# Natural order of the model dimension, and half of the input tiles transposed by DMA, in a fused spectral and GEGLU backward pass

## The chip, the cores and the metric

The kernel runs on one core of one Trainium2 chip. The metric is the device time of one execution in microseconds (us). The core has TensorE (PE in the profile, with its weight loads as PEld), VectorE (DVE), ScalarE (ACT), GpSimd (POOL) and SyncE (SP). SP computes nothing: it issues DMA transfers, one after the other in the order of the program. ACT and POOL issue some transfers too.

## The reference

The reference computes a gated mix of two branches and its gradients. x has 2048 rows (S) of 576 columns (D), F is 4608, all inputs are bf16.

```python
x = A_x
g = sigmoid((x * gate_w).sum(-1, keepdims=True))
a = irfft2(rfft2(x) * (w_r + 1j * w_i))             # over rows and columns
b = (gelu(x @ w_gate) * (x @ w_up)) @ w_down        # gelu with tanh
out = g * a + (1 - g) * b
```

It returns `out` and the gradients of `out` with respect to A_x, w_r, w_i, w_gate, w_up, w_down and gate_w for a given `grad_out` (dO). The reference names a second input B_x, on which nothing depends.

## The kernel before, in words

**Layout.** The 2048 rows stand as 16 row tiles (T) of 128 partitions; partition p holds rows 16p to 16p + 15. `xn` and `dB` hold x and dO as they are (128, 16, 576). `xT` and `dOT` hold them turned, (128, 5, 16, 128): chunk ci of row tile t has 128 of the 576 columns on the partitions. Chunks 0 to 3 are the first 512 columns; in chunk 4 the last 64 columns lie in the lower or upper half of the partitions, by the parity of the row tile.

**Order of the columns.** `eo(c)` says which columns are chunk c: every fourth one from c on, so partition p of chunk c holds column 4p + c. The weights follow: `load_w` loads w_gate and w_up with four neighbouring rows to a partition ("(p r) f -> p r f"). w_down is turned by a DMA transpose into `wtmp`, stored to DRAM (`wscr`) and loaded again in that order into `wdT`.

**Phase 1** loops over 18 groups g of 256 columns of F, and in each over four passes m of four row tiles (NPR = 4; a pass has the number pr = 4g + m). `H_mm` computes z = dO w_down^T (L456 and, for the last 64 columns, L461) and xy = x [w_gate, w_up] (L465 for the last 64, L472). ACT then copies and squares the halves of xy (`H_act`), and DVE and ACT make the gelu, its derivative and the products (`H_ew1`, `H_ew2`). Their results, A and dH, are stored for phase 2 and feed the weight gradients (`W_units`, L584, L602 and L616), which are worked off in the passes of the next group. From pass 7 on one or more units of the Fourier transform of x and of g dO are put between them (`fft_next`; L646 and L660 are its matmuls, Z and ve the copies out of PSUM). Tables for it are computed on the way: F over the columns (`build_F`), R over the rows (`build_R`), B between. Sines that are due late are collected in `tb.late` and run in pass 6 (`run_late`).

**Group 0** also makes `xT` and `dOT`. x and dO are loaded four row tiles at a time at the start of SP's queue. PE turns 128x128 blocks against an identity matrix (`titems`, L411 and L417; `pair`, L427) into PSUM, and ACT or DVE copies them out (L418, L428). Tiles 4 to 7 are turned in pass 0, 8 to 11 of dO in passes 0 and 1, and so on, always ahead of their use. `gate(k)` (L435) computes the gate for the row tiles of pass k from `xT`; it stands at the end of pass k - 1. The gate of pass k is used in `H_da`.

**SP's queue** in group 0 holds, in the order of the program: w_down's first rows, dO and x of tiles 0 to 3, w_gate and w_up of group 0, dO and x of tiles 4 to 15; then in pass 0 a small table of three rows, stored to DRAM (`kscr`, L110) and loaded back as a column (`kc`, L111), used in phase 2; then the weights of group 1 in parts (L345 to L357), spread over passes 0 to 2; then the stores of A and dH. A DMA waits on SP for what it needs, and all behind it wait too. PE, ACT and DVE too run their instructions in the order that the Python code writes out: the kernel has a manual schedule, and tile pools add the waits on buffers.

**Phase 2**, from 899 us on, loads A and dH back turned by DMA transposes (`pin`, L1133) and computes b and the gradient of x (L1207), the inverse transforms (L1260, L1270) and the outputs.

**Small buffers.** The tiles of the elementwise work come from the pool `ew`; the tags q, s and sg have one buffer there from group 1 on. 18 `unit` buffers in turn serve tables and transforms.

Of the kernel before, what the change touches and what calls it, by code (L numbers as in the profile page):

```python
# [9 lines left out]
ACT = mybir.ActivationFunctionType  # L10
# [18 lines left out]
FG = 256  # L29
# [12 lines left out]

def eo(c):

    return slice(c, 512, 4)


class Unit:
# [13 lines left out]
def iotas(nc, res, unit):  # L62
    tb = Tables()
    G, V = nc.gpsimd, nc.vector
    kw = dict(allow_small_or_imprecise_dtypes=True)
    tb.halfpi = res.tile([P, 1], F32, name="halfpi")
    V.memset(tb.halfpi[:], math.pi / 2)
    tb.pi = res.tile([P, 1], F32, name="pi")
    V.memset(tb.pi[:], math.pi * EPS_SCALE)
    tb.warm = res.tile([P, 1], F32, name="warm")  # L70
    nc.scalar.activation(tb.warm[:], tb.halfpi[:], ACT.Sin)
    tb.lrow = unit([LQ], F32, name="lrow")
    G.iota(tb.lrow[:], pattern=[[1, LQ]], base=0, channel_multiplier=0, **kw)
    tb.dcol = res.tile([P, 6], F32, name="dcol")
    for k, (r, step, n) in enumerate(((1, 1, 2), (0, 0, 1), (5, -1, 3))):
        k0 = (0, 2, 3)[k]
        G.iota(tb.dcol[:, k0:k0 + n], pattern=[[step, n]], base=r, channel_multiplier=6, **kw)
    tb.late = []
    tb.Rt = []
    return tb  # L80
# [39 lines left out]
def build_F(nc, tb, unit):  # L120

    V = nc.vector
    step = 2.0 * math.pi / D
    X = unit([6, LQ], F32, name="XF")
    y = unit([6, LQ], F32, name="yF")
    V.tensor_tensor(X[:], tb.dcol[:].unsqueeze(2).to_broadcast([P, 6, LQ]), tb.lrow[:].unsqueeze(1).to_broadcast([P, 6, LQ]), op=ALU.mult)
    V.tensor_scalar(y[:], X[:], 1.0 / D, MAGIC, op0=ALU.mult, op1=ALU.add)
    V.tensor_scalar(y[:], y[:], -MAGIC, -float(D), op0=ALU.add, op1=ALU.mult)
    V.tensor_tensor(X[:], X[:], y[:], op=ALU.add)
    V.scalar_tensor_tensor(y[:], X[:], -1.0, X[:], op0=ALU.mult, op1=ALU.max)  # L130
    tb.F = unit([6, 2, LQ], name="Ft")

    def sines():
        nc.scalar.activation(tb.F[:, :, 0], y[:], ACT.Sin, bias=tb.halfpi[:], scale=-step)
        nc.scalar.activation(tb.F[:, :, 1], X[:], ACT.Sin, scale=-step * EPS_SCALE)
    return sines


def build_I(nc, tb, ftile, small, out):
# [152 lines left out]
def kernel(  # L292
# [21 lines left out]
    o4v = out_4[0:512, :].rearrange("(c p) f -> p c f", p=P)  # L314
    o5v = out_5[0:512, :].rearrange("(c p) f -> p c f", p=P)
    scr = [[dram.tile([4, P, FF], BF16, name=f"scr{k}_{m}") for m in range(T // 4)] for k in range(3)]
    wscr = [dram.tile([512, FG], BF16, name=f"wscr{k}") for k in range(2)]
    scr_x = dram.tile([P, T, 2, DF], BF16, name="scr_x")
    scr_g = dram.tile([P, T, 2, DF], BF16, name="scr_g")
    kscr = dram.tile([3, P], F32, name="kscr")  # L320
# [10 lines left out]
    dB = wstack.enter_context(tc.tile_pool(name="pdB", bufs=1)).tile([P, T, D], BF16, name="dB")  # L331

    wts = {}
    wtmp = [None]

    def load_w(g, part, tails=LD):

        fsl = slice(g * FG, (g + 1) * FG)
        if g not in wts:
            wts[g] = (wpool.tile([P, 5, 2 * FG], BF16, tag="wgu", name="wgu"), wpool.tile([P, 5, FG], BF16, tag="wdT", name="wdT"))  # L340
        if part == 0:
            wgu = wts[g][0]
            for w, c0 in ((B_w_gate, 0), (B_w_up, FG)):
                cols = slice(c0, c0 + FG)
                LD.dma_start(wgu[:, 0:4, cols], w[0:512, fsl].rearrange("(p r) f -> p r f", r=4))  # L345
                for r in (LO, HI):
                    tails.dma_start(wgu[r, 4, cols], w[512:D, fsl])
        elif part == 1:
            wtmp[0] = wpool.tile([P, 4, FG], BF16, tag="wtmp", name="wtmp", bufs=1)
            LD.dma_start_transpose(wts[g][1][:, 4:5, :], B_w_down[fsl, DCH[4][0]:D])  # L350
            LD.dma_start_transpose(wtmp[0][:], B_w_down[fsl, 0:512])
        elif part == 2:
            wdT = wts[g][1]
            LD.dma_start(wdT[LO, 4, :], wdT[HI, 4, :])
            LD.dma_start(wscr[g % 2][:].rearrange("(c p) f -> p c f", p=P), wtmp[0][:])
        else:
            LD.dma_start(wts[g][1][:, 0:4, :], wscr[g % 2][:].rearrange("(p r) f -> p r f", r=4))  # L357

    def load_x(t0):
        LD.dma_start(xn[:, t0:t0 + 4, :], x_v[:, t0:t0 + 4, :])  # L360

    def load_do(t0, n=4):
        LD.dma_start(dB[:, t0:t0 + n, :], do_v[:, t0:t0 + n, :])
# [8 lines left out]
    load_do(2, 2)  # L372
    load_x(0)
    load_w(0, 0, nc.scalar)
    for k in range(1, 4):
        load_do(4 * k)
        load_x(4 * k)
    tb = iotas(nc, res, unit)

    ew = wstack.enter_context(tc.tile_pool(name="ew", bufs=2))  # L380
# [49 lines left out]
    def gate(k):  # L430
        lps = pgtile()
        ts = slice(4 * k, 4 * k + 4)
        for t in range(4 * k, 4 * k + 4):
            for ci in range(5):
                nc.tensor.matmul(lps[:, t:t + 1], lhsT=xT[:, ci, t, :], rhs=gwT[:, (ci, 4 + t % 2)[ci == 4]:][:, 0:1],  # L435
                                 start=(ci == 0), stop=(ci == 4))
        nc.scalar.activation(g_bf[:, ts], lps[:, ts], ACT.Sigmoid)
        nc.scalar.activation(omg_bf[:, ts], g_bf[:, ts], ACT.Identity, bias=1.0, scale=-1.0)
        nc.scalar.copy(omg32[:, ts], omg_bf[:, ts])
# [35 lines left out]

    def ewt(tag, g):
        if tag in ("q", "s", "sg"):
            return unit([4, FG], name=tag) if g == 0 else ew.tile([P, 4, FG], BF16, tag=tag, name=tag, bufs=1)
        return ew.tile([P, 4, FG], BF16, tag=tag, name=tag, bufs=2)

    def H_da(g, m, z):
# [5 lines left out]
    def H_act(k, xy, tiles, part):  # L487
        xb, q, hu = tiles
        h = slice(2 * k, 2 * k + 2)
        if part == 0:  # L490
            nc.scalar.activation(q[:, h, :], xy[:, :, 0:FG], ACT.Square)  # L491
        else:
            nc.scalar.copy(xb[:, h, :], xy[:, :, 0:FG])  # L493
            nc.scalar.copy(hu[:, h, :], xy[:, :, FG:2 * FG])  # L494
# [228 lines left out]
    def turned():  # L723
        tp_ = pftile(BF16)
        for v in range(2):
            nc.tensor.transpose(tp_[:, 0, v * P:(v + 1) * P], tb.B[:, v, :], ident[:])
        V.tensor_copy(tb.BT[:].rearrange("p v m -> p (v m)"), tp_[:, 0, 0:2 * P])  # L727

    def zipped(u1, u2):
        out = [u1[0]]  # L730
# [148 lines left out]
    for c in range(6):  # L879
        w = gwr[0:1, eo(c)] if c < 4 else gwr[0:1, 512:D]  # L880
        r = slice(0, P) if c < 4 else (LO, HI)[c - 4]
        nc.tensor.matmul(gps[r, c:c + 1], lhsT=w, rhs=one[:], start=True, stop=True)
    F0 = build_F(nc, tb, unit)
    AC(gwT[:, 0:4], gps[:, 0:4])
    for c, r in ((4, LO), (5, HI)):
        AC(gwT[r, c:c + 1], gps[r, c:c + 1])
    for f in titems(wdn, wts[0][1][:].rearrange("p k (c m) -> p k c m", c=2), 0, (phtile, pgtile, phtile), (VC, AC, VC), n=2):
        f()
    F0()
    pair(dB, dOT, 0, pgtile, VC)  # L890
    pair(dB, dOT, 2, pgtile, AC)
    titems(dB, dOT, 0, (None, None, phtile), (None, None, VC))[2]()
    nc.scalar.activation(tb.warm[:], tb.halfpi[:], ACT.Sigmoid)
    parity = iotas_R(nc, tb, res, unit, kscr)
    makeB = build_B(nc, tb, unit, res)

# [70 lines left out]

    wgT_from = 54

    carry, pend, held, rest = [], None, [], []  # L970

    def scale_dB(k, cp):
        for t in range(4 * k, 4 * k + 4):
# [5 lines left out]
    for g in range(NG):  # L979
# [3 lines left out]
        for m in range(NPR):  # L983
# [13 lines left out]
            def sigs(g=g, m=m, tiles=tiles, state=state):  # L997
                H_ew2(g, m, tiles, *state)
            if g == 0:
                def items(src, dst, t, *cp):  # L1000
                    return titems(src, dst, 4 * t, (pgtile,) * 3, cp) if t < NPR else [None] * 3
                do1 = items(dB, dOT, 1, VC, VC, VC) if m == 0 else []
                do2 = items(dB, dOT, m + 2, AC, AC, VC)
                x1 = items(xn, xT, m + 1, AC if m else VC, VC, VC)
                z, xy_full = H_mm(g, m, [lambda: gate(0)] if m == 0 else rest, opening if m == 0 else None)
                rest = []
                da = H_da(g, m, z)
                if m == 0:
                    early, mid_, late_ = do1[:2], [do1[2], x1[0]], x1[1:]
                elif m < NPR - 1:  # L1010
                    early, mid_, late_ = x1[:1], x1[1:], []
                else:
                    early, mid_, late_ = [], [], []
                for f in early:
# [19 lines left out]
                if m == 0:  # L1034
                    build_R(nc, tb, unit, 4)
                    columns_B(nc, tb, res)
                elif m == 1:
                    next(makeB)
                if m < NPR - 1:
                    gate(m + 1)  # L1040
                else:
                    V.tensor_copy(g32[:], g_bf[:])
                if m + 2 < NPR:
                    do2[0]()
                    rest = do2[1:]
                state += [*H_ew1(g, tiles, da), da]
                held.append(sigs)
            else:
# [7 lines left out]
                if held:  # L1056
                    scale_dB(0, AC)
                    held.pop()()
                for part in (1, 0):
                    H_act(0, xy, tiles, part)  # L1060
                k0 = int(n > 0 and pr > 6 and ready())
                pcopy[0] = VC
                xy = xy_full(1, fft_next if k0 else None)
                pcopy[0] = AC
                for part in range(2):
                    H_act(1, xy, tiles, part)
                if pr == 4:
# [38 lines left out]
                    sigs()  # L1106
            carry = []
            if m < 3 and g + 1 < NG:
                for part in ((0, 1), (2,), (3,))[m]:
                    load_w(g + 1, part)  # L1110
            if done[0] == n_slots or (pr >= wgT_from and pr % 2 == 0 and len(wgT_all) < 20):
                load_wgT()
# [344 lines left out]
```

## Time and profile before

| what | value |
|---|---|
| median of three runs | 1371.8 us (1371.41 to 1372.44) |
| the profiled execution's own time | 1371.81 us |
| its span in the profile | 1370.0 us, so 1.8 us lie around it |
| granted TensorE clock | 1.000 |
| PE / DVE / ACT / POOL busy in the span | 99% / 67% / 55% / 22% |
| group 0 of phase 1, passes 0 to 3 | from 8.2 to 44.7 us |
| phase 1 / phase 2 | to about 899 us / from there |
| DMA | 214 MB, mean 156 GB/s |

The times of the profile are counted from the start of the span. A row of the timeline gives start, duration, engine, line, operation, the tile that is written and the tiles that are read, shape, count, and in brackets the idle time ahead of it and what ended it. SPq, ACTq and POOLq are the queues' issuing instructions. A row of the waits gives who waited for whom, the sum in us, how many times, and the longest. A row of a tile's or a line's instructions gives the count, the least, median and greatest duration in ns, and the first and last start.

### The profile page before, as it was taken

To read this page: it belongs to the slowest core of one execution; us is meant where nothing else is said; L and a number is where in the kernel's file an instruction comes from. 1 tells how busy PE (TensorE), PEld (TensorE's weight loads), DVE (VectorE), ACT (ScalarE), POOL (GpSimd) and SP (SyncE) were. 2 spreads that over 40 slices of the span, in tenths; PEclk is the share of its full clock that TensorE was granted. 3 is DMA by queue.
4 is the path that set the end of the run, shared out by engine and by line. 5 is a ranking of instruction groups with operands and counts; after the bars stand their busy time and mean duration, and the time that the engine had idled before them with its cause. 6 is when DMAs were issued, how large, how long until landed. Compare 5 with 4: busy or idle time off the path is not lost.

```text
span 1370.0 us, 27201 instructions
## 1 busy us (share of the span) xinstructions
PE 1358.1 (99%) x10408; PEld 904.1 (66%) x10408; DVE 911.7 (67%) x2349; ACT 752.1 (55%) x1358; POOL 299.4 (22%) x508
## 2 busy tenths in 40 slices
PE   9999999999999999999999999999999999999999
PEld 7556656556556656655655555658888888888887
DVE  7899999999867876876786655526536443545320
ACT  7886767767667767676776666522332322223210
POOL 3012234342213532532442211100000000000000
PEclk9999999999999999999999999999999999999999
DMA  7435445454545645644755648599999778789773
GB/s 228 124 95 138 114 143 148 137 135 137 156 131 141 185 113 140 184 128 130 198 141 147 168 120 186 125 232 228 211 215 205 174 156 165 168 159 174 155 148 75
DMA packets 498553, 214.25 MB, mean 156 GB/s; under 512 B 307347, under 2 KB 488278, under 8 KB 498422
## 3 DMA queue, kind: packets, MB, share of 16 engines
q1 hardware_dynamic: 472084, 177.66, 55.7%
q0 software_dynamic: 14912, 24.24, 6.1%
q10 hardware_dynamic: 11426, 10.61, 3.2%
q8 instruction: 81, 1.33, 0.4%
q14 instruction: 50, 0.41, 0.1%
HBM read 45.49 MB, written 93.56 MB: 101 GB/s over the span
## 4 chain that ended last, share of the span: by engine, by line
PE 76%; DVE 1%; issue 0%; ACT 0%; DVEq 0%
PE acc L1207 31%; PE wps L602 13%; PE xy L472 12%; PE wps L584 7%; PE z L456 6%; PE wps L616 2%; PE xy L465 1%; PE z L461 1%; PE acc L1260 1%; PE acc L1270 1%; PE pf L848 1%; PE pf L770 1%; PE pf L646 0%; PE pf L660 0%; DVE sd L668 0%
## 5 line engine op out<-in xcount | busy, mean ns | idle before, releaser
L1207 PEld LDWEIGHTS <-pin 128*128 128x128 bf16 x3456 | 334.8, 98 | 83.2 <-issue 1.1
L472 PE MATMUL xy<-wgu,xT 128*128 128x512 bf16 x1152 | 270.7, 380 | 0.0
L602 PE MATMUL wps<-dH,xn 128*128 128x512 bf16 x1152 | 265.7, 379 | 0.0
L602 PEld LDWEIGHTS <-xn 128*128 128x128 bf16 x1152 | 111.0, 98 | 125.1 <-issue 0.6
L472 PEld LDWEIGHTS <-xT 128*128 128x128 bf16 x1152 | 105.8, 98 | 131.9 <-issue 24.8
L609 POOL DMA_DIRECT2D out_dram<-dw x134 | 73.8, 554 | 396.8 <-ACT dw L553 379.3
L584 PE MATMUL wps<-dB,A 128*128 128x288 bf16 x1152 | 149.8, 286 | 0.3 <-ACT dwd L553 0.3
L1207 PE MATMUL acc<-wd_all,pin 128*128 128x288 bf16 x1152 | 146.7, 286 | 0.0
L1207 PE MATMUL acc<-wgT,pin 128*128 128x288 bf16 x1152 | 146.6, 286 | 0.0
L1207 PE MATMUL acc<-wuT,pin 128*128 128x288 bf16 x1152 | 146.0, 286 | 0.0
L1272 ACT ACTIVATE yo<-acc 128x288 bf16<-128x288 f32 x64 | 67.5, 1247 | 133.6 <-PE acc L1270 114.6
L456 PE MATMUL z<-wdT,dOT 128*128 128x256 bf16 x1152 | 137.7, 273 | 0.8 <-DVE BTtab L727 0.7
L584 PEld LDWEIGHTS <-A 128*128 128x128 bf16 x1152 | 112.0, 98 | 33.8 <-issue 0.5
L484 ACT ACTIVATE da<-z,omg 128x256 bf16<-128x256 f32 x288 | 112.0, 472 | 33.8 <-PE z L461 33.6
L1388 DVE TENSOR_TENSOR b16t<-acc,f32t 128x288 bf16<-128x288 f32 x32 | 14.6, 458 | 171.7 <-PE acc L1207 171.7
L456 PEld LDWEIGHTS <-dOT 128*128 128x128 bf16 x1152 | 112.4, 98 | 22.5 <-issue 1.0
L493 ACT CAST xb<-xy 128x512 bf16<-128x512 f32 x144 | 85.2, 591 | 48.7 <-PE xy L472 48.7
L491 ACT ACTIVATE q<-xy 128x512 bf16<-128x512 f32 x144 | 88.0, 613 | 16.6 <-DVE s L536 10.2
L494 ACT CAST hu<-xy 128x512 bf16<-128x512 f32 x144 | 87.5, 608 | 0.0
L1262 ACT CAST Z<-acc 98x384 bf16<-98x384 f32 x64 | 27.5, 481 | 105.6 <-PE acc L1260 105.6
L530 DVE TENSOR_TENSOR xb<-xb,sg 128x1024 bf16<-128x1024 bf16 x48 | 32.9, 685 | 70.7 <-ACT sg L522 70.7
L553 ACT CAST dw<-wps 128x512 bf16<-128x512 f32 x72 | 42.3, 589 | 63.9 <-PE wps L602 62.9
(516 smaller groups left out, 1876.1 us busy)
## 6 DMA issues: line engine op xcount, KB each, us to landing
scr<-dH SPq DMA_DIRECT2D x144, 256.0 KB, 3.5
scr<-A SPq DMA_DIRECT2D x72, 256.0 KB, 2.5
out_dram<-dw POOLq DMA_DIRECT2D x134, 64.0 KB, 1.9
wd_all<-in_B_w_down_dram SPq DMA_DIRECT2D x3, 1728.0 KB, 11.1
out_dram<-dwd POOLq DMA_DIRECT2D x34, 144.0 KB, 3.1
scr_p<-Vt SPq DMA_DIRECT2D x32, 144.5 KB, 2.6
Vp<-scr_p ACTq DMA_DIRECT2D x32, 144.5 KB, 4.1
wgu<-in_B_w_gate_dram SPq DMA_DIRECT2D x18, 256.0 KB, 4.5
```

Of the source, the lines that this page charges most:

```text
L456: nc.tensor.matmul(zo(t), lhsT=dOT[:, ci, t, :], rhs=wdT[:, ci, :], start=(t % 4 < 2 and ci == 0), stop=False)
L472: nc.tensor.matmul(xy[k][:, t % 2, :], lhsT=xT[:, ci, t, :], rhs=wgu[:, ci, :], start=False, stop=(ci == 3))
L484: nc.scalar.activation(da[:, t, :], z[:, t % 2, t // 2, :], ACT.Copy, scale=omg32[:, 4 * m + t:4 * m + t + 1])
L491: nc.scalar.activation(q[:, h, :], xy[:, :, 0:FG], ACT.Square)
L493: nc.scalar.copy(xb[:, h, :], xy[:, :, 0:FG])
L494: nc.scalar.copy(hu[:, h, :], xy[:, :, FG:2 * FG])
L553: wcopy[0](out, in_)
L584: nc.tensor.matmul(wps[:, :288], lhsT=tl(0, t)[:, fch * P:(fch + 1) * P], rhs=dB[:, t, h * 288:(h + 1) * 288], start=(t == 0), stop=(t == ...
L602: nc.tensor.matmul(wps[:].rearrange("p a b -> p (a b)"), lhsT=xn[:, t, c * P:(c + 1) * P], rhs=kt[t // 4][1][:, t % 4].rearrange("p k f -> ...
L609: wst[0].dma_start(ov[:, c, fsl], dw[:, k, :])
L1207: nc.tensor.matmul(acc[:, :288], lhsT=src[:, r, :], rhs=w_of(r)[:, h * 288:(h + 1) * 288], start=(first and r == 0), stop=(last and r == F ...
L1272: nc.scalar.activation(yv[:, 3 * b:3 * b + 3], ps[:, 0:288].rearrange("p (r q) -> p r q", r=3), ACT.Copy, scale=(SD2, 1.0)[w])
```

## The change

Four edits and some small ones come together.

- **Natural order.** `eo(c)` is now columns 128c to 128c + 127. The weights are loaded with "(r p) f -> p r f", w_down's DMA transpose goes straight into `wdT`, and `wtmp`, `wscr` and the two transfers through DRAM are gone. The half-partition copy of `wdT` stays, in pass 1.
- **Eight tiles by DMA.** Row tiles 8 to 15 of dO and x come into `dOT` and `xT` by DMA transposes from the inputs in DRAM, two for each tile and input, 32 in all. They are issued on SP right behind the loads of tiles 4 to 7. The plain loads of x for tiles 8 to 15 come behind them; those of dO move to the ends of passes 1 and 2. The 80 PE transposes of these tiles and their copies are gone. Tiles 0 to 7 stay on PE.
- **Late D table.** `build_F` moves from the start to pass 3, and its two sines to the late tables of pass 6. ACT starts with the sigmoid table instead of the sine table, so one table load falls away.
- **Second buffer for the square** of the gelu (tag q), from group 1 on.
- **Pieces ahead of the square.** In groups 1 to 17 the square of the first half (`H_act(0, ..., 0)`) now stands behind the second half's matmuls, and so behind the copy of the transform's unit between them.
- The copy of the table BT out of PSUM goes from DVE to ACT.

```diff
 def eo(c):
-    return slice(c, 512, 4)
+    return slice(c * P, (c + 1) * P)
...
-    nc.scalar.activation(tb.warm[:], tb.halfpi[:], ACT.Sin)
+    nc.scalar.activation(tb.warm[:], tb.halfpi[:], ACT.Sigmoid)
...
-    return sines
+    tb.late.append(sines)
...
-                LD.dma_start(wgu[:, 0:4, cols], w[0:512, fsl].rearrange("(p r) f -> p r f", r=4))
+                LD.dma_start(wgu[:, 0:4, cols], w[0:512, fsl].rearrange("(r p) f -> p r f", p=P))
...
-            wtmp[0] = wpool.tile([P, 4, FG], BF16, tag="wtmp", name="wtmp", bufs=1)
             LD.dma_start_transpose(wts[g][1][:, 4:5, :], B_w_down[fsl, DCH[4][0]:D])
-            LD.dma_start_transpose(wtmp[0][:], B_w_down[fsl, 0:512])
-        elif part == 2:
-            wdT = wts[g][1]
-            LD.dma_start(wdT[LO, 4, :], wdT[HI, 4, :])
-            LD.dma_start(wscr[g % 2][:].rearrange("(c p) f -> p c f", p=P), wtmp[0][:])
+            LD.dma_start_transpose(wts[g][1][:, 0:4, :], B_w_down[fsl, 0:512])
         else:
-            LD.dma_start(wts[g][1][:, 0:4, :], wscr[g % 2][:].rearrange("(p r) f -> p r f", r=4))
+            LD.dma_start(wts[g][1][LO, 4, :], wts[g][1][HI, 4, :])
...
-    for k in range(1, 4):
-        load_do(4 * k)
-        load_x(4 * k)
+    load_do(4)
+    load_x(4)
+    for t0 in (8, 12):
+        for v, dst in ((grad_out, dOT), (A_x, xT)):
+            flat = v[0].rearrange("(p t) d -> p (t d)", t=T)
+            for t in range(t0, t0 + 4):
+                LD.dma_start_transpose(dst[:, 0:4, t, :], flat[:, t * D:t * D + 512])
+                c0 = t * D + (512, D - P)[t % 2]
+                LD.dma_start_transpose(dst[:, 4:5, t, :], flat[:, c0:c0 + P])
+    load_x(8)
+    load_x(12)
     tb = iotas(nc, res, unit)
...
-            return unit([4, FG], name=tag) if g == 0 else ew.tile([P, 4, FG], BF16, tag=tag, name=tag, bufs=1)
+            return unit([4, FG], name=tag) if g == 0 else ew.tile([P, 4, FG], BF16, tag=tag, name=tag, bufs=1 + (tag == "q"))
...
-        V.tensor_copy(tb.BT[:].rearrange("p v m -> p (v m)"), tp_[:, 0, 0:2 * P])
+        AC(tb.BT[:].rearrange("p v m -> p (v m)"), tp_[:, 0, 0:2 * P])
...
-    F0 = build_F(nc, tb, unit)
...
-    F0()
...
-    nc.scalar.activation(tb.warm[:], tb.halfpi[:], ACT.Sigmoid)
...
-                do1 = items(dB, dOT, 1, VC, VC, VC) if m == 0 else []
-                do2 = items(dB, dOT, m + 2, AC, AC, VC)
-                x1 = items(xn, xT, m + 1, AC if m else VC, VC, VC)
-                z, xy_full = H_mm(g, m, [lambda: gate(0)] if m == 0 else rest, opening if m == 0 else None)
+                do1, x1 = ([titems(src, dst, 4, (pgtile,) * 3, (VC,) * 3) for src, dst in ((dB, dOT), (xn, xT))]
+                           if m == 0 else ([], []))
+                z, xy_full = H_mm(g, m, [lambda: gate(0)] if m == 0 else [], opening if m == 0 else None)
...
+                elif m == 3:
+                    build_F(nc, tb, unit)
...
-                if m + 2 < NPR:
-                    do2[0]()
-                    rest = do2[1:]
+                if m in (1, 2):
+                    load_do(4 * m + 4)
...
-                for part in (1, 0):
-                    H_act(0, xy, tiles, part)
                 k0 = int(n > 0 and pr > 6 and ready())
+                xy0 = xy
+                H_act(0, xy0, tiles, 1)
                 pcopy[0] = VC
                 xy = xy_full(1, fft_next if k0 else None)
                 pcopy[0] = AC
+                H_act(0, xy0, tiles, 0)
...
-                for part in ((0, 1), (2,), (3,))[m]:
+                for part in ((0, 1), (2,), ())[m]:
                     load_w(g + 1, part)
```

More of the change, by code (lines that the diff above doesn't have):

```diff
@@ L316 @@
     scr = [[dram.tile([4, P, FF], BF16, name=f"scr{k}_{m}") for m in range(T // 4)] for k in range(3)]
-    wscr = [dram.tile([512, FG], BF16, name=f"wscr{k}") for k in range(2)]
     scr_x = dram.tile([P, T, 2, DF], BF16, name="scr_x")
@@ L333 @@
     wts = {}
-    wtmp = [None]
     def load_w(g, part, tails=LD):
@@ L968 @@
     wgT_from = 54
-    carry, pend, held, rest = [], None, [], []
+    carry, pend, held = [], None, []
     def scale_dB(k, cp):
@@ L999 @@
             if g == 0:
-                def items(src, dst, t, *cp):
-                    return titems(src, dst, 4 * t, (pgtile,) * 3, cp) if t < NPR else [None] * 3
-                do1 = items(dB, dOT, 1, VC, VC, VC) if m == 0 else []
-                do2 = items(dB, dOT, m + 2, AC, AC, VC)
-                x1 = items(xn, xT, m + 1, AC if m else VC, VC, VC)
-                z, xy_full = H_mm(g, m, [lambda: gate(0)] if m == 0 else rest, opening if m == 0 else None)
-                rest = []
+                do1, x1 = ([titems(src, dst, 4, (pgtile,) * 3, (VC,) * 3) for src, dst in ((dB, dOT), (xn, xT))]
+                           if m == 0 else ([], []))
+                z, xy_full = H_mm(g, m, [lambda: gate(0)] if m == 0 else [], opening if m == 0 else None)
                 da = H_da(g, m, z)
@@ L1009 @@
                     early, mid_, late_ = do1[:2], [do1[2], x1[0]], x1[1:]
-                elif m < NPR - 1:
-                    early, mid_, late_ = x1[:1], x1[1:], []
                 else:
```

## The prediction

> **What bounds the kernel now.** I read the page first, for the busy shares.
>
> ```profile
> PE 1358.1 (99%) x10408; PEld 904.1 (66%) x10408; DVE 911.7 (67%) x2349; ACT 752.1 (55%) x1358; POOL 299.4 (22%) x508
> ```
>
> A busy PE says little by itself, since matmuls are pipelined. So I read next who PE waited for, once over the first 51 us and once over the rest. These are the four longest of the rest:
>
> ```profile
> PE pf L646 <- ACT Z L649: 1.3, 1, 1.3
> PE pf L660 <- ACT Z L651: 1.2, 2, 0.7
> PE pf L660 <- ACT Z L649: 1.0, 2, 0.5
> PE z L456 <- DVE BTtab L727: 0.7, 1, 0.7
> ```
>
> All seven waits of that list sum to 5.2 us in 1319 us. From 51 us on, PE has no real slack: time that is lost or won ahead of 51 us is kept to the end, and the edits further on can win a few us at most. The question is therefore the opening, and there I read the timeline of PE around row group 0 (four passes over four row tiles each, then group 1):
>
> ```profile
> 1.36 3.38 PE L877 MATMUL pf<-ident 128*128 128x128 bf16 x30 [1.36 <-POOL ident masks.py:199]
> 18.91 0.62 PE L411 MATMUL pf<-ident,dB 128*128 128x128 bf16 x8
> 27.39 0.64 PE L435 MATMUL pf<-gwT,xT 128*128 128x1 bf16 x20
> 35.78 0.61 PE L411 MATMUL pf<-ident,xn 128*128 128x128 bf16 x8 [1.64 <-DVE dOT L418]
> 38.17 0.64 PE L435 MATMUL pf<-gwT,xT 128*128 128x1 bf16 x20
> 46.58 0.39 PE L461 MATMUL z<-wdT,dOT 64*128 64x256 bf16 x4
> ```
>
> The two L435 rows are gate(2) and gate(3), the first uses of xT tiles 8 to 11 and 12 to 15. The row at 46.58 is the tail of z in pass 0 of group 1: the first work that needs the whole wdT of group 1. I use it as the marker. The last view is SP's queue in the same stretch, and what a DMA transpose costs on it:
>
> ```profile
> 8.39 0.33 SPq L363 DMA_DIRECT2D dB<-in_grad_out_dram  x1
> 12.21 0.30 SPq L110 DMA_DIRECT2D kscr<-kr  x1
> 17.91 0.40 SPq L111 DMA_DIRECT2D kc<-kscr  x1
> 18.37 0.57 SPq L345 DMA_DIRECT2D wgu<-in_B_w_gate_dram  x1
> 22.79 1.26 SPq L350 DMA_TRANSPOSE wdT<-in_B_w_down_dram  x1
> 24.11 1.29 SPq L351 DMA_TRANSPOSE wtmp<-in_B_w_down_dram  x1
> 29.76 0.34 SPq L357 DMA_DIRECT2D wdT<-wscr  x1
> ```
> ```profile
> L350 SPq DMA_TRANSPOSE wdT<-in_B_w_down_dram x17: 1197/1259/1644, 22.8 to 815.8; - x17
> L351 SPq DMA_TRANSPOSE wtmp<-in_B_w_down_dram x17: 1287/1322/2522, 24.1 to 817.5; - x17
> ```
>
> The columns of the last two are min/median/max in ns. A plain load holds SP for 0.3 to 0.6 us, a transpose for 1.2 to 1.3, and it hardly matters how much it moves: L350 turns 256x128 elements, L351 256x512, for 5% more time. It is a price per instruction.
>
> **The change part by part.** *Eight tiles by DMA.* Removed from PE: tiles 8 to 15 of x and dO, five transposes each, 80 in all. Eight take 0.62 us of which the last one's end is 0.22, so (0.62 - 0.22)/7 = 57 ns each, 4.6 us together; the 1.6 us wait on a dOT copy goes with them. Their copies out of PSUM leave ACT and DVE. Without anything else the marker would come 6.2 us earlier, at 40.4.
>
> Added to SP: 32 transposes (L374 and L376 of the changed kernel), from the place of the load at 8.39, which waits for the same landing. The price c of one, start to start, is 1.32 (24.11 - 22.79). The shapes are 128 rows by 512 or 128, so smaller than L351 and L350; I take 1.30, with 1.24 (the least L350 and a 0.04 gap) and 1.46 (the 1.41 median of the larger pin transposes at L1133, and a gap) as the ends. 32 x 1.30 = 41.6, from 8.4 to 50.0. Landing takes 3.8 us from issue (medians of 3.8 to 4.0 for both transposes).
>
> - xT tile 11 is the 16th: 8.4 + 15 x 1.3 + 3.8 = 31.7. PE reaches gate(2) at 27.4 less 40 transposes, about 25. It waits 6.6 us.
> - From gate(2) to gate(3) was 10.8; less 40 transposes and the 1.6 us wait, 6.9. PE is there at 38.6, and tile 15 lands at 8.4 + 31 x 1.3 + 3.8 = 52.5. It waits 14 us. Behind gate(3) stand all matmuls of pass 3, since PE runs in order. Pass 3 took 6.6 us (38.17 to 44.74), so PE wants group 1 at 59, or at 61 with the clock below.
>
> *What the transposes are put ahead of on SP.* The loads of xn 8 to 15 (0.9 us, to 50.9), then kscr (0.3), then kc, which waits for kscr to land. In the profile that took 5.3 us behind four loads of 576 KB; a 1 KB store of the POOL queue lands in 2.7. Here two such loads are ahead: I take 4.0, with 2.7 and 5.3 as ends. kc 0.4, the six wgu loads 4.3 (18.37 to 22.79 was 4.4; the next group's took 4.0): 59.9. Then the two wdT transposes: the main one starts at 61.2 and lands at 65.0; the tail's lands at 63.9, and only then can wdT be copied to its other half (L350 of the changed kernel; 32 KB, median 3.5 to land): 67.4. The added load of dB 8 to 11 sits ahead of that copy but has issued by then.
>
> So the marker moves from 46.58 to 67.4: **+20.8 us**. In one line: 8.4 + 32c + 9.9 + 4.0 + 3.5, which equals the old 46.58 at c = 0.65.
>
> *Clock.* The 30 opening matmuls start 106 ns apart ((3.38 - 0.31)/29), where the transposes at 18.91 start 57 apart, so PE begins slow. Granted clock is 1.00 in the page's rows and does not show this. PE would stand idle for about 4 us ahead of group 1: +1, between 0 (it stays quick) and 2.5 (half of the some 5 us after 1.36 in which rows are slow).
>
> The Trainium skill, "TensorE: Matmul & The Clock Gate", Part 1, says that PE falls to half clock after an idle window of some 3.4 us and needs as long to recover; by it the term would be 1.7 at most. No wait of that length is in this trace.
>
> *Natural order, no wscr.* Shapes and counts stay; transposes from strided (L411) and plain columns (L417) both average 219 ns. The second and third trip of wdT (17 x 0.5 MB each way) go. DMA is 0.4 to 0.6 busy there and PE waits for no weights after 51 us: 0 now. In group 1 the two trips are already left out of the chain above.
>
> *Late D table.* Five DVE operations (0.47, 0.59, 0.89, 0.47, 0.47: 2.9 us) go from the first 5 us to pass 3, where DVE was busy 5.84 of 6.1 us. PE's wait for the weights covers them; without that cover 0 to +2.9. Two sines (1.0 us on ACT) go to the run of late tables in pass 6, where ACT is busy 41 of 49 us: 0, or +1. A table load (1.28 us at 8.92) goes; ACT then waited for PE anyway: 0.
>
> *Pieces ahead of the square, second q buffer, BT copy on ACT.* The copy of Z or ve comes out one square (0.61 us) earlier, and the 10 us that ACT waited for q go. PE gains only where it waited for such a copy: between 0 and the 4.5 us of Z, ve and BT in its list. The square of the first half now ends later, but its PSUM buffer is wanted only after the weight-gradient matmuls: 0. I take -1.5, a third, since a PE wait right behind the matmul that feeds the copy stays.
>
> **Sum:** 20.8 + 1.0 - 1.5 = +20.3 on the profiled execution's 1371.81, which is the median of the runs too (1371.8): 1392.
>
> The Trainium skill, "Advanced Engine Details and Errata", X-Bar Transpose (TRN2), says that transposing DMAs are as fast as regular ones. For bytes that may hold; on SP's queue the rows above say 1.26 against 0.3 to 0.6. At 0.5 each the chain would end at 42, under the marker's old place, and the forecast would be some 5 us faster than before. The measured rows decide.
>
> **The rivals.** *Transposes paced by their bytes.* If SP's 1.3 us were only waiting for room in the queue, they would go at the pace of the first six pin transposes, 6 x 384 KB in 13.2 us, 178 GB/s: 2.6 MB in 14.7 us, c = 0.46. The chain gives 40.6, PE is the bound again at 40.4, and the gains stand: 1371.8 - 6.2 - 1.5 = 1364. It decides from c below 0.65. Against it: no transpose in the trace holds SP for less than 1.197, at four different sizes. 10%.
>
> *Transposes stretched by traffic.* The longest L351 held SP for 2.52 while stores were under way. If the 16 large ones do, that adds 16 x 1.2 = 19 us: 1411. For it: loads are in flight at 8.4; against it: DMA would be nearly idle from some 15 us on. 5%.
>
> *The delay is made good later, or tiles land in time:* within 0.2% (2.7 us, about what a measurement of this kernel can tell from none). PE would need 18 us of slack behind 51 us, and the list has 5.2. 2%.
>
> **How the numbers follow.** The forecast has 83%. Its own ends: low, c 1.24 (-1.9), kscr 2.7 (-1.3), copy landing in 2.2 (-1.3), clock 0 (-1), all of the 4.5 us won (-3): 1384; high, c 1.46 (+5.1), kscr 5.3 (+1.3), clock 2.5 (+1.5), copy 5.2 (+1.7), late tables +1: 1403. I widen the low side a little, for waits of which I see only one execution: 1380 to 1404. Faster 10%, same 2%, slower 88%.
>
> **What would show it.** Right: 32 transposes on SP at 1.2 to 1.4 us each from about 8 to 50 us; PE's list with waits at L435 or L436 on DMAs into xT of some 6 and 14 us; a wait of some 4 us at z of group 1 on wdT; the stretch from 51 us on unchanged to within 5 us. Wrong: transposes spaced under 0.7 us, PE reaching gate(3) before 40 us, or PE waits of more than 5 us elsewhere.

## The result, and the profile after

| | before | after |
|---|---|---|
| median | 1371.93 us (1371.41 to 1372.44, 4 runs) | 1389.88 us (1389.29 to 1393.24, 4 runs) |
| the profiled execution's own time | 1371.81 us | 1390.39 us |
| its span | 1370.0 us | 1388.6 us |
| the marker (tail of z, pass 0 of group 1) | 46.58 us | 69.25 us |
| from the marker to the end | 1323.4 us | 1319.4 us |

The ratio is 1.0137, 95% interval 1.0124 to 1.0149: 1.4% slower. The span grew by 18.6 us. The last two rows split that: the opening lost 22.7 us, and the rest won 4.1.

The page after, busy shares first, then the granted clock over the 40 slices:

```profile
PE 1360.1 (98%) x10328; PEld 902.1 (65%) x10328; DVE 903.8 (65%) x2342; ACT 749.1 (54%) x1351; POOL 299.0 (22%) x508
...
PEclk9699999999999999999999999999999999999999
```

PE has 80 matmuls fewer. Its busy share fell by one point only, as the new waits (22.2 us) are 1.6% of the span. The clock row has changed: it was 9 in all slices before, and the second slice (35 to 69 us) now has 6.

SP's queue in the opening, from its timeline (start, duration, operation):

```profile
8.66 1.29 SPq L374 DMA_TRANSPOSE dOT<-in_grad_out_dram  x1
9.99 1.23 SPq L376 DMA_TRANSPOSE dOT<-in_grad_out_dram  x1
11.26 1.83 SPq L374 DMA_TRANSPOSE dOT<-in_grad_out_dram  x1
...
19.59 2.39 SPq L374 DMA_TRANSPOSE xT<-in_A_x_dram  x1
...
50.44 1.23 SPq L376 DMA_TRANSPOSE xT<-in_A_x_dram  x1
51.72 1.05 SPq L353 DMA_DIRECT2D xn<-in_A_x_dram  x2
52.88 0.30 SPq L110 DMA_DIRECT2D kscr<-kr  x1
57.18 0.40 SPq L111 DMA_DIRECT2D kc<-kscr  x1
57.63 0.47 SPq L343 DMA_DIRECT2D wgu<-in_B_w_gate_dram  x1
...
62.52 1.30 SPq L348 DMA_TRANSPOSE wdT<-in_B_w_down_dram  x1
...
64.55 0.51 SPq L350 DMA_DIRECT2D wdT<-wdT  x1
```

The 32 transposes run from 8.66 to 51.7 us, 1.35 us each from start to start. The small ones (128x128) hold SP for 1.23, the large ones (128x512) for 1.26, but for three. The first took 1.29. The one of 1.83 stands where the loads of tiles 4 to 7 were still landing. The one of 2.39 does not: DMA moved 14 GB/s from 19.6 to 22.0 us, and what held it is not known. The weights of group 1, which began at 18.4 us before, begin at 57.6.

Who PE waited for, over the whole span:

```profile
PE pf L436 <- DMA xT<-in_A_x_dram: 17.4, 13, 3.8
PE z L457 <- DMA wdT<-in_B_w_down_dram: 4.8, 1, 4.8
PE pf L878 <- POOL ident masks.py:199: 1.4, 1, 1.4
PE pf L647 <- ACT ve L667: 0.5, 1, 0.5
PE pf L647 <- ACT da L485: 0.5, 1, 0.5
PE acc L1192 <- ACT dw L554: 0.5, 1, 0.5
```

Two long waits are new, both on SP's transfers: the gates on xT, and z on the wdT of group 1. The waits on Z and BT, 4.2 us before, are gone.

The rows of PE's timeline that answer to those of before:

```profile
32.02 0.43 PE L436 MATMUL pf<-gwT,xT 128*128 128x1 bf16 x5 [2.26 <-DMA xT<-in_A_x_dram]
52.87 0.19 PE L436 MATMUL pf<-gwT,xT 128*128 128x1 bf16 x1 [0.63 <-DMA xT<-in_A_x_dram]
65.73 3.59 PE L457 MATMUL z<-wdT,dOT 128*128 128x256 bf16 x16 [4.78 <-DMA wdT<-in_B_w_down_dram]
69.25 0.61 PE L462 MATMUL z<-wdT,dOT 64*128 64x256 bf16 x4
```

The first two are the ends of gate(2) and gate(3). The third is z in pass 0 of group 1: 16 matmuls in 3.59 us. The same 16 in the kernel before:

```profile
44.74 1.91 PE L456 MATMUL z<-wdT,dOT 128*128 128x256 bf16 x16
```

The busy times by stretch point to the clock (start and end, length, then busy us of PE, PEld, DVE, ACT and POOL, then granted clock, DMA share and GB/s):

```profile
40.50:53.00 12.50, 1.75 (x21) 1.18 (x22) 5.65 (x10) 1.51 (x3) 0.00 (x0) 0.60 0.31 65
65.70:69.30 3.60, 3.57 (x18) 2.24 (x20) 3.43 (x9) 0.00 (x0) 0.00 (x0) 0.50 0.88 288
```

After PE had stood idle for 4.8 us, it was granted half of its clock. DMA was far from full while the gate waited: 65 GB/s.

### The profile page after: what moved, and what is told of

It reads as the page before. It is cut to its first block, busy times and chain, and to the rows that moved or that the text cites. A ratio compares the mean times of both kernels' runs of the same rounds, so it can differ in the third digit from the quotient of the medians.

```text
span 1388.6 us, 27004 instructions
## 1 busy us (share of the span) xinstructions
PE 1360.1 (98%) x10328; PEld 902.1 (65%) x10328; DVE 903.8 (65%) x2342; ACT 749.1 (54%) x1351; POOL 299.0 (22%) x508
## 4 chain that ended last, share of the span: by engine, by line
PE 94%; SPq 3%; DMA 1%; ACT 1%; issue 0%; ACTq 0%; DVE 0%
PE acc L1201 31%; PE wps L603 18%; PE xy L473 17%; PE wps L585 10%; PE z L457 9%; PE wps L617 2%; PE xy L466 2%; SPq L374 2%; PE z L462 2%; SPq L376 1%; PE pf L647 1%; PE acc L1254 1%; PE pf L661 1%; PE acc L1264 1%; PE pf L849 1%; PE pf L771 1%
## 5 line engine op out<-in xcount | busy, mean ns | idle before, releaser
L457 PE MATMUL z<-wdT,dOT 128*128 128x256 bf16 x1152 | 142.7, 279 | 4.8 <-DMA wdT<-in_B_w_down_dram 4.8
L1266 ACT ACTIVATE yo<-acc 128x288 bf16<-128x288 f32 x64 | 67.4, 1246 | 132.1 <-PE acc L1264 124.6
L492 ACT ACTIVATE q<-xy 128x512 bf16<-128x512 f32 x144 | 80.3, 602 | 3.6 <-PE xy L473 3.2
L531 DVE TENSOR_TENSOR xb<-xb,sg 128x1024 bf16<-128x1024 bf16 x48 | 32.9, 686 | 70.6 <-ACT sg L523 70.6
```

The source lines that it names most:

```text
L457: nc.tensor.matmul(zo(t), lhsT=dOT[:, ci, t, :], rhs=wdT[:, ci, :], start=(t % 4 < 2 and ci == 0), stop=False)
L1266: nc.scalar.activation(yv[:, 3 * b:3 * b + 3], ps[:, 0:288].rearrange("p (r q) -> p r q", r=3), ACT.Copy, scale=(SD2, 1.0)[w])
```

## The experiments

The theory after the result: a DMA transpose costs a fixed time on SP, and what stands behind the 32 on that queue, the weights of group 1, sets the loss; the gain behind it comes from ACT's copies. Rivals: the transposes go by their bytes or by the traffic; the loss comes from another edit; the slow z is no matter of the clock. Eleven kernels were run. Each ratio compares with the kernel before on the same chip; its median was 1371.7 to 1373.6 us, so that times from two chips can differ by up to 2 us without a cause in the kernel.

### One part undone: all tiles on PE again

```diff
-    load_do(4)
-    load_x(4)
-    for t0 in (8, 12):
-...
+    for k in range(1, 4):
+        load_do(4 * k)
+        load_x(4 * k)
...
-                if m in (1, 2):
-                    load_do(4 * m + 4)
+                if m + 2 < NPR:
+                    do2[0]()
+                    rest = do2[1:]
```

> The changed kernel with one part undone: row tiles 8 to 15 are turned on PE again and all plain loads stand at the start of SP's queue as before; natural order, no trip through DRAM, late D table, second q buffer, pieces ahead of the square and the BT copy on ACT stay. Theory (the price of a DMA transpose on SP is the whole loss, the other edits win about 4 us after 51 us): 1367 to 1369 us, and the tail of z in pass 0 of group 1 at about 46 us. Rival (some of the loss comes from another edit, such as the new row order of the weight loads or the late table): above 1372.

Measured: 1370.2 us (1368.4 to 1373.4, 11 runs), ratio 0.9981 (0.9971 to 0.9991); marker at 46.22. The sign and the place are those of the theory: the transposes, with what they push back on SP, are the whole loss. The time is 1 to 3 us longer than the 1367 to 1369 that was expected. The waits show where:

```profile
PE wps L595 <- DVE dH L533: 1.9, 1, 1.9
PE acc L1200 <- DMA pin<-scr: 1.8, 2, 1.6
```

The first stands at 58 us, right behind the five table operations that the late D table put on DVE in pass 3 (50.6 to 52.7 us). The kernel after has that work too (67.0 to 69.1 us), but there PE is late itself, and its list has no wait on DVE. The second is in phase 2, and the runs differ in it. From marker to end this profile has 1323.1 us; less the two waits that is 1319.4, as in the kernel after.

### Fewer instructions, the same bytes

```diff
-                LD.dma_start_transpose(dst[:, 0:4, t, :], flat[:, t * D:t * D + 512])
-                c0 = t * D + (512, D - P)[t % 2]
-                LD.dma_start_transpose(dst[:, 4:5, t, :], flat[:, c0:c0 + P])
+                n = (5, 4)[t % 2]
+                LD.dma_start_transpose(dst[:, 0:n, t, :], flat[:, t * D:t * D + n * P])
+                if t % 2:
+                    LD.dma_start_transpose(dst[:, 4:5, t, :], flat[:, (t + 1) * D - P:(t + 1) * D])
```

> The changed kernel with the two transposes of each even row tile joined in one of 640 columns (its chunk 4 is the next 128 columns in DRAM), so 24 instructions on SP in place of 32 with the same bytes. Theory (a price per instruction of 1.28 us, with the weights of group 1 behind them): eight fewer, 10.2 us earlier, 1379 to 1381 us; a joined one holds SP for 1.26 to 1.35 us. Rival (the transposes go at the pace of their bytes, or the loads' landing bounds it): 1388 to 1390, a joined one as long as the two it replaces, 2.5 us.

Measured: 1382.1 us (1380.5 to 1383.6, 4 runs), ratio 1.0074 (1.0060 to 1.0087), 1.1 us above the range of the theory and far from that of the rival. The transposes' rows of dO, in ns (least, median, most):

```profile
L375 SPq DMA_TRANSPOSE dOT<-in_grad_out_dram x8: 1258/1275/1876, 8.4 to 30.8; - x8
L377 SPq DMA_TRANSPOSE dOT<-in_grad_out_dram x4: 1230/1230/1231, 11.1 to 32.1; - x4
...
59.12 0.39 PE L463 MATMUL z<-wdT,dOT 64*128 64x256 bf16 x4
```

Half of the eight in the first row have 640 columns, half 512. Taken one by one, the undisturbed ones held SP for 1.28 to 1.30 us with 640 columns and for 1.26 to 1.27 with 512: two that are joined cost as little as one. The last row, from the timeline, is the marker: 10.1 us earlier, as expected for eight fewer. Of it 2 us were lost again behind the marker, and this profile has 2.1 us of waits on pin in phase 2 that the kernel after had not. The price goes by the instruction, not by the bytes.

### What stands behind them: kc from another queue

```diff
-        nc.sync.dma_start(kscr[:].rearrange("(o k) m -> o k m", o=1), kr[0:1])
-        nc.sync.dma_start(tb.kc[:], kscr[:].rearrange("k m -> m k"))
+        G.dma_start(kscr[:].rearrange("(o k) m -> o k m", o=1), kr[0:1])
+        G.dma_start(tb.kc[:], kscr[:].rearrange("k m -> m k"))
```

> The changed kernel with the store of kscr and the load of kc issued from POOL in place of SP, so that nothing waits on SP for kscr to land. Theory (SP's order is the chain): the 4.75 us from the issue of kscr to that of the next wgu load go; the weights of group 1 land at about 61 us, when PE is ready at 60.6, so that z may also run at the full clock (1.9 in place of 3.6 us): 1383.5 to 1385.5 us. Rival (the loads of xn ahead hold the DMA engines, so that the weights land no earlier): 1389 to 1390.

Measured: 1386.1 us (1385.7 to 1386.5, 4 runs), ratio 1.0102 (1.0087 to 1.0118). From SP's and PE's timeline:

```profile
51.06 1.05 SPq L353 DMA_DIRECT2D xn<-in_A_x_dram  x2
52.16 0.43 SPq L343 DMA_DIRECT2D wgu<-in_B_w_gate_dram  x1
...
56.04 1.68 SPq L347 DMA_TRANSPOSE wdT<-in_B_w_down_dram  x1
57.77 2.71 SPq L348 DMA_TRANSPOSE wdT<-in_B_w_down_dram  x1
...
62.09 1.92 PE L457 MATMUL z<-wdT,dOT 128*128 128x256 bf16 x16 [1.65 <-DMA wdT<-in_B_w_down_dram]
65.06 0.39 PE L462 MATMUL z<-wdT,dOT 64*128 64x256 bf16 x4 [1.04 <-DMA wdT<-wdT]
```

The marker came 4.2 us earlier, so SP's order is the chain. That is 0.6 us less than the 4.75 that was expected to go, and the time is 0.6 us above the range given: part of the wait came back as longer transposes of wdT (1.68 and 2.71 in place of 1.25 and 1.30). They now follow the loads of xn closely; that these stretch them was not tried by itself. After a wait of 1.65 us z ran in 1.92 us.

### The clock

```diff
             else:
+                if pr == NPR:
+                    warm = ph.tile([P, 2, 2 * FG], F32, tag="xy", name="xy")
+                    for _ in range(16):
+                        nc.tensor.matmul(warm[:, 0, :], lhsT=ident[:], rhs=xT[:, 0, 0:4, :], start=True, stop=True)
                 z, xy_full = H_mm(g, m)
```

> The changed kernel with 16 matmuls of 512 columns, whose result nobody reads, put ahead of z in pass 0 of group 1, into PE's wait of 4.8 us for wdT. Theory (the 1.7 us by which that z was longer, 3.6 in place of 1.9 us, are the clock, granted at 0.50 after the wait): granted clock near 1.0 there, z in 1.9 to 2.1 us, the marker at 67.6 to 68.0 in place of 69.25 us, 1388 to 1389 us. Rival (z is slow because its operands are fresh or DMA is busy, 0.88 to 1.1 of 16 engines): z stays at 3.6 us, 1390.

Measured: 1390.0 us (1389.1 to 1390.7, 4 runs), ratio 1.0118 (1.0103 to 1.0134). From the busy times by stretch, and PE's timeline:

```profile
65.70:69.30 3.60, 1.91 (x16) 1.55 (x16) 3.40 (x8) 0.00 (x0) 0.00 (x0) 1.00 0.90 284
```
```profile
65.95 1.91 PE L457 MATMUL z<-wdT,dOT 128*128 128x256 bf16 x16 [1.06 <-DMA wdT<-in_B_w_down_dram]
69.45 0.39 PE L462 MATMUL z<-wdT,dOT 64*128 64x256 bf16 x4 [1.59 <-DMA wdT<-wdT]
```

Of the expectation, the clock half was right: granted 1.00, z in 1.91 us. The time half was wrong: the marker stayed (69.45, where 67.6 to 68.0 was expected). It is the marker that decides here: the kernel before had a median of 1373.6 us on this chip, 1.7 more than in the first comparison, so the times cannot tell 1 us. A wait of 1.59 us for the other half of wdT took the place of the slow z. That copy was issued at 64.48 and let PE go at 69.45. In the kernel after it was issued at 64.55 and took 4.3 us to land, to 68.9, under cover of the slow matmuls. So the two are parallel there, and the slow clock alone can cost the marker no more than the 0.4 us from 68.9 to 69.25.

### Where the gain behind the marker comes from

Three kernels, all from the one with the tiles on PE. The first puts the square back ahead of the pieces:

```diff
-                k0 = int(n > 0 and pr > 6 and ready())
-                xy0 = xy
-                H_act(0, xy0, tiles, 1)
+                for part in (1, 0):
+                    H_act(0, xy, tiles, part)
+                k0 = int(n > 0 and pr > 6 and ready())
                 pcopy[0] = VC
                 xy = xy_full(1, fft_next if k0 else None)
                 pcopy[0] = AC
-                H_act(0, xy0, tiles, 0)
```

> As pe_tiles (1370.2 us), but with the square of the first half back ahead of the transform's pieces; the second q buffer stays. pe_tiles had PE wait 1.0 us for copies of Z or ve from 51 us on, the kernel before 3.8. Theory A (ACT held the copies back because its square waited for the one q buffer): with two buffers the order hardly matters, waits of at most 1.6 us, 1370 to 1371 us. Rival B (the order is the gain, one square of 0.6 us ahead of each copy): waits of 3 to 4 us, 1372.5 to 1373.5 us.

The second has one q buffer:

```diff
-...name=tag, bufs=1 + (tag == "q"))
+...name=tag, bufs=1)
```

> As pe_tiles, but with one q buffer; the pieces stay ahead of the square. Theory A (the square's wait for the buffer held the copies back): the copies are ahead of the square now, so 1370 to 1371 us, though ACT waits some 10 us for q again. Rival C (that wait on ACT reaches PE by another way, through the PSUM of xy or the copies of weight gradients): 1372 us or more, with PE waits on ACT that pe_tiles has not.

The third has both:

> As pe_tiles, with both undone: the square ahead of the pieces and one q buffer, as before. Both theories: PE's waits for Z and ve come back to 3.5 to 4 us, 2.8 more than in pe_tiles: 1372.5 to 1373.5 us. If it stays at 1370 to 1371, the few us won behind 51 us in the changed kernel come from neither.

| kernel | median (range), 11 runs each | ACT waits on q's buffer |
|---|---|---|
| tiles on PE | 1370.2 us (1368.4 to 1373.4) | none |
| square first, two buffers | 1369.2 us (1368.2 to 1370.2) | none |
| pieces first, one buffer | 1370.7 us (1370.3 to 1371.3) | 6.3 us |
| square first, one buffer | 1372.8 us (1372.3 to 1373.2) | 10.2 us |

ACT's wait for q's buffer with one buffer, pieces first and then square first, and PE's waits with both undone:

```profile
ACT q L484 <- DVE s L529: 6.3, 5, 2.5
...
ACT q L484 <- DVE s L529: 10.2, 6, 3.0
...
PE pf L653 <- ACT Z L644: 1.2, 2, 0.7
PE pf L653 <- ACT Z L642: 1.0, 2, 0.5
PE pf L639 <- ACT Z L642: 0.9, 1, 0.9
```

PE's waits are back where the kernel before had them. Either edit alone takes away most of them (0.3 us of waits for Z and ve is left with two buffers, 1.2 with the pieces first), as theory A has it: ACT's square stood and waited for the one q buffer, and the copy that PE needed stood behind it. A second buffer frees the square; another order takes the copy past it. The two together win 2.5 us by the medians, 3.6 by the ratios to the kernel before (0.9981 against 1.0007; tiles on PE ran on another chip than the other three). The second buffer alone wins as much or more (3.6 us by the medians, a time 0.8 below what was expected), the order alone 2.1, and the order adds nothing to the second buffer that these runs can show. The share of the BT copy (0.7 us of wait in the profile before) was not tried by itself.

### A version that is faster than both

Only tiles 12 to 15 by DMA, even ones joined, so 12 instructions, behind the loads of tiles 8 to 11:

```diff
+    load_do(8)
+    load_x(8)
+    for v, dst in ((A_x, xT), (grad_out, dOT)):
+        flat = v[0].rearrange("(p t) d -> p (t d)", t=T)
+        for t in range(12, T):
+            n = (5, 4)[t % 2]
+            LD.dma_start_transpose(dst[:, 0:n, t, :], flat[:, t * D:t * D + n * P])
+            if t % 2:
+                LD.dma_start_transpose(dst[:, 4:5, t, :], flat[:, (t + 1) * D - P:(t + 1) * D])
+    load_do(12)
+    load_x(12)
```

> As pe_tiles, but row tiles 12 to 15 come by DMA transposes (12 instructions, even tiles joined), behind the loads of tiles 8 to 11; x's first. Theory (only the place in SP's queue matters; 12 x 1.28 = 15.4 us end at about 25 us, and the weights of group 1 land at about 39 us, ahead of PE at about 42): the 40 PE transposes saved, 2.3 us, show: 1363.5 to 1367 us, 2 to 4 us under pe_tiles. Rival (any transposes in the opening cost, by traffic or by delayed loads): at or above pe_tiles.

Measured: 1368.4 us (1367.3 to 1372.2, 7 runs), ratio 0.9976 (0.9965 to 0.9987); marker at 43.57. PE waits for none of the transposed tiles, and the marker is 2.7 us ahead of that of the kernel with all tiles on PE. By the medians the time is 1.9 us under that kernel, just short of the 2 to 4 expected, and 1.4 us above the 1367 that was expected at most; the ranges of the two kernels overlap. The wait of 1.9 us on DVE at 58 us is still there. Two kernels move the table that causes it: first ahead of the dO copies, then ahead of all copies.

```diff
-                elif m == 3:
-                    build_F(nc, tb, unit)
...
+    build_F(nc, tb, unit)
     pair(dB, dOT, 0, pgtile, VC)
```

> As dma4 (1368.4 us), but the five DVE operations of the D table stand ahead of the first dO copies, where DVE waits for loads, and only the two sines are late. pe_tiles and dma4 have PE wait 1.9 us for a product of DVE at 58 us, right behind the five operations in pass 3. Theory (the late table's 2.0 us on DVE cause it): that wait goes, 1366 to 1367 us. Rival (DVE would be late there anyway): 1368 us.

Measured: 1368.1 us (1366.3 to 1369.2, 6 runs). The wait at 58 us went, and another came at 7.7:

```profile
PE z L459 <- DVE dOT L431: 1.7, 1, 1.7
```

A miss of the 1366 to 1367 expected: DVE was needed there too.

```diff
+    build_F(nc, tb, unit)
     AC(gwT[:, 0:4], gps[:, 0:4])
```

> As dma4_f_mid (1368.1 us), but the five DVE operations of the D table stand ahead of the first copies of w_down's rows, where DVE has nothing to do until about 5.5 us. In dma4_f_mid the 1.9 us wait at 58 us was gone, but PE waited 1.7 us at 7.7 us for a dO copy behind the table. Theory (only the place on DVE matters): neither wait is there, 1366 to 1367 us. Rival (the wait turns up at a third place): 1368 us.

Measured: 1367.3 us (1366.4 to 1368.7, 5 runs), ratio 0.9957 (0.9944 to 0.9969). Neither wait on DVE is left, but PE now is early for the weights, so that a wait did turn up at a third place, as the rival had it:

```profile
PE z L459 <- DMA wdT<-in_B_w_down_dram: 2.0, 1, 2.0
...
42.69 1.92 PE L459 MATMUL z<-wdT,dOT 128*128 128x256 bf16 x16 [2.03 <-DMA wdT<-in_B_w_down_dram]
```

The last kernel adds kc from POOL, the edit shown above.

> As dma4_f_first (1367.3 us), with the store of kscr and the load of kc issued from POOL. There PE waited 2.0 us at 40.3 us for the wdT of group 1, and SP stood 4.0 us for kscr. Theory: the weights of group 1 land some 2 to 4 us earlier and PE's wait goes, marker at about 42.5 in place of 44.5 us: 1365 to 1366 us. Rival (the transposes of wdT stretch behind the loads of tiles 12 to 15, as they did by 1.8 us in kc_pool): 1367 us.

Measured: 1365.9 us (1365.8 to 1366.2, 5 runs), ratio 0.9957 (0.9943 to 0.9970): 6 us under the kernel before and 24 under the kernel after. No wait on wdT is left; 1.7 us of waits on ACT's work on xy, in pass 3 and just behind it, took its place, so that the marker moved by 0.3 us only (44.54 to 44.22, where 42.5 was expected). The ratio is that of the kernel without this edit, so these runs don't show that the edit wins time.

## Why the prediction was right, point by point

1392 was forecast, 1380 to 1404 as the range; 1389.9 came.

- **The price on SP.** Right. 1.30 us was taken, 1.35 measured: 1.23 and 1.26 with their gaps, and two of 1.83 and 2.39. The transposes ended at 51.7 (50.0 forecast); tile 15 let PE go at 52.9 (52.5), since its last one took 2.4 us to land in place of 3.8. These two errors offset each other, which is luck. The run with 24 of them shows the price to be one per instruction, so the rival of bytes falls; that of stretching by traffic shows in one transpose, at 0.6 us in place of 19.
- **The gates.** Waits of 6.6 and 14 us were forecast. Measured were 6.6, in five pieces as the transposes landed, and 10.9 in eight (17.4 in the list together). PE came to gate(3) at 40.4 in place of 38.6, as pass 2 ran at a granted clock of 0.76 (32.3 to 40.5 us), z in 3.57 us. None of this reached the end, since the weights came later still.
- **What stands behind on SP.** kc waited 4.0 us (4.0 forecast); the wgu loads took 3.6 (4.3). z could start at 65.7 (65.0); the weights' chain began 2.0 us later than forecast and made up 1.3 in the loads and the landing. With kc on POOL 4.2 us went from the marker: the term is real.
- **The last link.** The copy of the half of wdT was put at 3.5 us after its issue, and it decides the marker in the forecast. Here the step was off: the copy was issued 0.65 us later than forecast and took 4.3 us to land (68.9 in place of 67.4), 5.0 in the run with the filler. The added load of dB, which the forecast called harmless, was issued 0.7 us ahead of it in both; but with kc on POOL, where that load also stood ahead of it, the copy let PE go after 3.3 us, so the cause stays open. In the kernel after it was covered by the slow z.
- **The clock.** +1 was taken on top of the copy; z lost 1.7 us (3.59 against 1.91). The Trainium skill's "TensorE: Matmul & The Clock Gate", Part 1, has PE at half clock after an idle window of about 3.4 us, and the granted clock of 0.50 after 4.8 us of idling agrees with it. The forecast's estimate from that page, 1.7 us at most, holds up to the marker; behind it the granted clock is still 0.57 from 69.3 to 70.6 us, so the whole loss is somewhat larger. But the term should not have been added in full: it runs beside the copy's landing, as the filler run showed, and put the marker only 0.4 us behind it. Copy and clock together moved the marker to 69.25, against 67.4 and +1 in the forecast: 0.9 us too little.
- **The gain behind.** -1.5 was taken out of 0 to -4.5, and -4.1 came. The term that was mis-sized is this one: a third was taken because a wait behind the matmul that feeds the copy would stay. It hardly did: 0.5 us is left on ve and none on Z and BT, where the list before had 4.5. The copies had been late because ACT stood waiting for q's buffer, 10 us that the forecast names in the same item; it counted only a third of PE's waits for these copies as won. The runs account for 2.5 to 3.6 of the 4.1 us by the two edits; the rest, with BT's copy, is not shown by a run of its own.
- **Late table.** It cost PE no wait in this kernel, as forecast. With the tiles on PE it cost a wait of 1.9 us, within the 0 to 2.9 that was given.
- **The page's rule.** That transposing DMAs are as fast as regular ones (the Trainium skill's "Advanced Engine Details and Errata", X-Bar Transpose (TRN2)) does not hold here for the time on SP: 1.23 to 1.30 against 0.3 to 0.6 us. The measured rows decided, as the forecast had said.

In sum: 22.7 - 4.1 = 18.6 us, where 21.8 - 1.5 = 20.3 was forecast. The opening was put 0.9 us too low and the gain 2.6 us too low, and the two errors offset part of each other: the chain on SP was right, and part of the closeness of the sum is luck.

## What to carry to other kernels

Count DMA instructions, not bytes, where a queue issues many of them: the 32 DMA transposes saved PE work of 4.6 us by the forecast's estimate, and cost the queue 43. Then follow that queue to the first thing behind them that the engine which sets the time needs, and see whether what is taken away there is covered by something parallel. Twelve transposes that fit into the queue's idle time brought the marker 2.7 us forward; the fastest kernel with them is 0.4% under the kernel before, part of which comes from the q buffer.

## What the runs showed of the hardware

- A DMA transpose held SP for 1.23 us at 128x128, 1.26 at 128x512 and 1.28 at 128x640. Stretched ones took 1.83 us with loads of 576 KB landing, and 2.39 at 14 GB/s without any; two together took 5.40 in one run (dma4_f_first, at 9.2 us, DMA at 400 GB/s).
- After a wait of 4.8 us, and after 6.6 and 10.9 us of waits broken by the short gate matmuls, PE was granted half its clock, and the next 16 matmuls of z took 3.57 to 3.59 us in place of 1.91. After single waits of 1.65 and 2.03 us they took 1.92.
- A 32 KB copy from one half of the partitions to the other took 4.3 us to land (kernel after), 5.0 from issue to use (run with the filler) and 3.3 (kc on POOL), each time with a 576 KB load issued 0.7 to 1.2 us ahead of it.
